# A decode kernel with two attention passes: K loads reordered behind the last fresh V, and the softmax bias from one row maximum

## The chip, the cores and the metric

The kernel runs on one core of a Trainium2 chip. The metric is device time in microseconds of one execution, as the median of the runs. A profile of one execution gives the trace that the numbers below come from. The engines are named as in the profile: PE (matrix multiply) with PEld (its weight loads), DVE (vector), ACT (scalar), POOL (GpSimd), and SP, whose queue issues the DMAs.

## What is computed

Four tokens (batch 4, one position each, width 448) go through attention over a cached window, then a gated feed-forward, and both once more with the same weights and the same cache:

```python
x = A_x
x = x + _A_ref(_layernorm(x, axis=-1), A_k_cache, A_v_cache, A_wq, A_wo)
x = x + _B_ref(_layernorm(x, axis=-1), B_w_gate, B_w_up, B_w_down)
x = x + _A_ref(_layernorm(x, axis=-1), A_k_cache, A_v_cache, A_wq, A_wo)
x = x + _B_ref(_layernorm(x, axis=-1), B_w_gate, B_w_up, B_w_down)
```

In the attention, 16 query heads of 256 share 8 KV heads, and the window is the last 2048 positions of the cache:

```python
scores = jnp.einsum("bhqd,bhkd->bhqk", q, k) * (Dh ** -0.5)
p = _softmax(scores, axis=-1)
o = jnp.einsum("bhqk,bhkd->bhqd", p, v)
```

So one KV head of one token is 1 MB of K and 1 MB of V, and there are 32 such heads, to be read for layer 0 and again for layer 1 (the second pass).

## The kernel before

**Pairs.** The unit of work is a "pair" (token `t`, layer, KV head): 64 in all, numbered by `pos`. `orders()` and `steps()` interleave the second pass of a token with the first pass of the next token. The end of the list is: 52 is (3, 0, 7), the last one of layer 0; 53 to 55 are (2, 1, 0), (2, 1, 1), (2, 1, 2); 56 to 60 are (3, 1, 3) to (3, 1, 7); 61 to 63 are (3, 1, 0), (3, 1, 1), (3, 1, 2).

**Cells.** K and V of a pair come in two halves of 512 KB, each in one of `NPOOL` = 27 cells `half`. The last five heads of each token in layer 0 keep their K and V in the cells for the second pass (`KEEP_K`, `KEEP_V`), so 20 cells are held while a token waits for its second pass, and its other three heads are loaded again.

**One pair** runs as follows. A K half lands (L722) and is transposed in place by DVE (L727). PE computes the scores into PSUM bank S (L748), 104 rows by 128. Each row holds one of two query heads by the parity of the row, and rows between the groups are empty. DVE takes each row's maximum (L759), PE spreads the 104 maxima over all rows by a matmul (L762: the maxima as weights, 32 columns of the identity as data), DVE takes the maximum over even and over odd columns, negated (L766, two values), and multiplies these with a parity mask and sums them into the bias of this row (L770, one instruction with an accumulator, which the profile shows as two). ACT takes the exponential with that bias (L773), PE turns the weights (L783), ACT copies them (L790), PE and DVE sum them (L793, L798), PE multiplies by V (L806, 16 matmuls, in two groups of 8 by V half, loaded by L735), POOL takes the reciprocal of the sum (L816), ACT and DVE join two parts (L818, L820), PE flips them (L826), DVE scales them (L831), and PE applies the output projection (L850 when a token is complete, else L858).

**Between the layers**, a complete token goes through `rows` (ACT L652, DVE L654, PE L662, DVE L666), `residual` (L670), `norm` (DVE L436 and L439, PE L442, DVE L446 to L455, POOL L459 to L463), the feed-forward (`ffn_row` from L558, or `ffn` with L612, L623 to L629 and L639), again `norm`, and `qproj`: L496 (two groups for each half of the result), ACT L502, PE L512 in two turns, DVE L519 (the copy qS), PE L527, DVE L532 (the query copy qc), then POOL builds the masked query of a pair (L752).

**Order.** Every operation is entered into a graph with an engine, a planned duration and a due time (`rank`), and `Graph.schedule` makes one fixed order for each engine. It always takes, of the operations ready by its own planned times, the one with the earliest due time. A DMA into a cell takes the cell that comes free first, and waits for the operation that frees it. Due times matter here in three places: a K half has `pos - KLEAD` (2.2), a V half `pos + VLAG` (1.3), and the work between the layers has `pos - CROSS` (20). On the chip each engine then runs its list in order, and waits on semaphores for what other engines produce.

The planner's own times only decide the order; they are not times of the chip.

Of the kernel before, what the change touches and what calls it, by code (L numbers as in the profile page):

```python
# [5 lines left out]
ACT = mybir.ActivationFunctionType  # L6
ALU = mybir.AluOpType
AX = mybir.AxisListType
# [5 lines left out]
B = 4  # L14
# [16 lines left out]

KLEAD = 2.2
VLAG = 1.3
SLEAD = 2.5
# [4 lines left out]
NS = 2  # L39
# [5 lines left out]
ROWF = (0, 1, 2)  # L45
MMV = 0.034
TAIL = {"pe": 0.2, "dve": 0.12, "act": 0.15, "pool": 0.1, "sp": 0.05}

# [231 lines left out]
def build(nc, A_x, A_k_cache, A_v_cache, A_wq, A_wo, B_x, B_w_gate, B_w_up, B_w_down, out):  # L280
# [3 lines left out]
    with ExitStack() as es:  # L284
        def sb(name, shape, dt):
            return es.enter_context(nc.sbuf_tensor(name, shape, dt))
# [9 lines left out]
        onesb, qmask, osel, rsel = tiny[:, 0:1], tiny[:, 2:6], tiny[:, 6:8], tiny[:, 8:12]  # L296
        pmax = [tiny[:, 12 + s:13 + s] for s in range(NS)]
        tsel = sb("tsel", [128, 4, B], BF16)
        selt = [sb(f"selt{h}", [128, 2, 4, 2, 2], BF16) for h in range(2)]
        small = sb("small", [128, 11 + 6 * NS + 4 * NY + B + 4], FP32)  # L300
        rmask = small[:, 11 + 6 * NS + 4 * NY:11 + 6 * NS + 4 * NY + B]
        rvec = small[:, 11 + 6 * NS + 4 * NY + B:11 + 6 * NS + 4 * NY + B + 4]
        nmask = small[:, 9 + 2 * NS + 4 * NY:11 + 2 * NS + 4 * NY]
        nbias = small[:, 11 + 2 * NS + 4 * NY:11 + 6 * NS + 4 * NY]
        onesf, wrow, lomask = small[:, 0:1], small[:, 1:5], small[:, 5:6]
# [71 lines left out]
        for h in range(2):  # L377
# [5 lines left out]
        g.op(DVE, 0.2, R0, lambda e: e.tensor_reduce(  # L383
            nmask[:, :], idq[:, :, 0:4, :].rearrange("p q a n -> p n q a"), AX.XY, ALU.add), r=("identb",), w=("nmask",))
        for s_ in range(NS):
            g.op(DVE, 0.2, R0, lambda e, s_=s_: e.memset(Sb[s_][:, :], 0.0), w=(f"s{s_}",), bank=(f"S{s_}",))
            g.op(DVE, 0.2, R0, lambda e, s_=s_: e.memset(praw[s_][:, :], 0.0), w=(f"praw{s_}",))
# [44 lines left out]
        def norm(t, rank, x):  # L432
# [24 lines left out]
            def gp(emit, r, w, dur=0.25):  # L457
                g.op(POOL, dur, rank, emit, r=r, w=w)
# [3 lines left out]
               (k + "m", k + "e", k + "w", k + "v"), (k + "h",))  # L462
            gp(lambda e: e.tensor_tensor(s[:, 8:9], s[:, 5:6], expo[:, 0:1], op=ALU.pow), (k + "h", "expo"), (k + "r2",))  # L463

# [243 lines left out]
        seq = [p for s in steps() for p in s]  # L708
        assert len(seq) == 2 * B * HKV and len(set(seq)) == len(seq)
        k_held, v_held = {}, {}  # L710
        done = {}
        pos = -1

        def pair(pos, si, side, nside, t, layer, kvh):
            p_, s_, q_ = pos % NY, pos % NS, pos % NQ
            if layer == 1 and (t, kvh) in k_held:
                kc, kk = k_held.pop((t, kvh))
            else:
                kc, kk = [[], []], [f"k{pos}_{hf}" for hf in range(2)]
                ksrc = A_k_cache[t, kvh, s0:s0 + WIN, :].rearrange("(p j) d -> p (j d)", p=128)  # L720
                for hf, cell in enumerate(kc):
                    g.dma(pos - KLEAD, 1 << 19, lambda e, cell=cell, hf=hf: e.dma_start(  # L722
                        half[cell[0]][:, :], ksrc[:, 2048 * hf:2048 * hf + 2048]), None, w=(kk[hf],), run=4096, cell=cell)

                    def tr(e, cell=cell):
                        a = half[cell[0]][:, :].bitcast(UINT32).rearrange("p (k s) -> p k s", k=32)
                        return e.transpose(a, a)  # L727
                    g.op(DVE, 1.18, pos, tr, w=(kk[hf],))
# [12 lines left out]
            def scores(e):  # L741
# [13 lines left out]
                r=(f"qc{t}_{kvh}",) + tuple(f"qmask{a}" for a in range(4)), w=(f"qe{q_}",))  # L755
            o = g.op(PE, 0.8, pos - SLEAD, scores, r=tuple(kk) + (f"qe{q_}",), w=(f"s{s_}",), bank=(f"S{s_}",))
            if not keep_k:
                o.rel = tuple(kc)
            g.op(DVE, 0.21, pos, lambda e: e.tensor_reduce(  # L759
                pmax[s_][0:104, :], Sb[s_][0:104, 0:128], AX.X, ALU.max),  # L760
                r=(f"s{s_}",), w=(f"pmax{s_}",), bank=(f"S{s_}",))
# [8 lines left out]
            g.op(DVE, 0.2, pos, lambda e: e.scalar_tensor_tensor(  # L770
                out=nb[0:104, 2:4], in0=negm[s_][0:104, :], scalar=1.0, in1=nmask[0:104, :], op0=ALU.mult, op1=ALU.mult,
                accum_out=nb[0:104, 0:1]), r=(f"negm{s_}", "nmask"), w=(f"nb{s_}",))
# [45 lines left out]
            g.op(SCA, 0.28, pos, lambda e: e.activation(oh[pos % 2][:, :], Yb[p_][:, 256:512], ACT.Copy), r=(f"y{p_}",),  # L818
                 w=(f"oh{pos % 2}",), bank=(f"Y{p_}",))
            g.op(DVE, 0.4, pos, lambda e: e.scalar_tensor_tensor(  # L820
                out=oh[pos % 2][:, :], in0=oh[pos % 2][:, :], scalar=lomask[:, 0:1], in1=Yb[p_][:, 256:512], op0=ALU.mult,
                op1=ALU.subtract), r=(f"y{p_}", f"oh{pos % 2}", "lomask"), w=(f"oh{pos % 2}",), bank=(f"Y{p_}",))

            def flip(e):
# [5 lines left out]
            o_ = oT[si % 2]  # L830
            g.op(DVE, 0.09, pos, lambda e: e.tensor_tensor(  # L831
                o_[:, :, :, t], Yb[p_][:, 0:4].rearrange("p (d n) -> p d n", n=2),
# [138 lines left out]
```

## Time and profile before

| what | us |
|---|---|
| median of 13 runs | 325.72 (322.11 to 328.94) |
| the profiled execution | 327.79 |
| its span, first to last instruction | 325.7 |
| busy: PE, PEld, DVE, ACT, POOL | 224.3, 136.0, 212.3, 74.9, 88.9 |
| moved by DMA | 105.16 MB, mean 323 GB/s |

The page shows the span in 40 slices of 8.14 us; a digit is the busy share in tenths, PEclk the clock that PE was granted, GB/s what the DMA engines moved:

```profile
PE   1746464556368757679779757785887688779775
DVE  7396645663255669877567769876778875845432
PEclk9999999999998787757675875576958755557655
GB/s 281 361 402 393 392 398 394 394 396 325 350 395 292 309 390 394 346 396 392 386 203 348 404 400 363 380 371 400 263 342 344 403 386 394 192 72 254 4 1 2
```

Transfers run near 390 GB/s for most of the span and drop at four places; the last five slices move next to nothing. PE runs at full clock at first and often at half of it later. The costliest groups (line, engine, operation, out and in, count, then busy us, mean ns of one, then the idle time before them and what ended it) begin with:

```profile
L727 DVE STREAM_TRANSPOSE half<-half 128x1024 uint32<-128x1024 uint32 x88 | 108.9, 1238 | 21.7 <-DMA half<-in_A_k_cache_dram 21.3
L806 PE MATMUL Y<-half,pT 128*4 128x256 bf16 x1024 | 62.1, 356 | 24.3 <-DMA half<-in_A_v_cache_dram 17.4
L748 PE MATMUL S<-half,qe 128*8 128x128 bf16 x2048 | 58.2, 278 | 6.3 <-DVE half L727 3.1
```

One transpose takes 1.24 us of DVE, which is long beside most other instructions there. The mean durations of PE overlap, as matmuls are pipelined.

### The profile page before, as it was taken

The page shows a single profiled execution, that of the slowest core. Times are in us where ns is not written, and L with a number is a line of the kernel's source. Part 1 is how long each engine was busy: PE and PEld are TensorE (multiplying, and loading weights), DVE is VectorE, ACT ScalarE, POOL GpSimd, SP SyncE. Part 2 cuts the span into 40 slices and gives each one's busy share as a digit, 9 for nine tenths or more (in the row PEclk, how much of TensorE's full clock was granted, in tenths as well). Part 3 has the DMA queues.
Part 4 walks back from the last instruction along what each step waited for, and adds up shares of the span by engine and source line. Part 5 has one row for each costly group of instructions (what it writes and reads, how often), then busy time and mean ns, then how long its engine had stood idle before and what let it go on. Part 6 is the DMA issues. An engine that isn't in the chain of part 4 may idle for free.

```text
span 325.7 us, 11153 instructions
## 1 busy us (share of the span) xinstructions
PE 224.3 (69%) x4776; PEld 136.0 (42%) x4776; DVE 212.3 (65%) x776; ACT 74.9 (23%) x222; POOL 88.9 (27%) x227
## 2 busy tenths in 40 slices
PE   1746464556368757679779757785887688779775
PEld 0334232223134435344346544443455446346444
DVE  7396645663255669877567769876778875845432
ACT  0122112111013223213232323131323322023210
POOL 1613211113010333223214323322243323225220
PEclk9999999999998787757675875576958755557655
DMA  7999999999997899999969999999799999526000
GB/s 281 361 402 393 392 398 394 394 396 325 350 395 292 309 390 394 346 396 392 386 203 348 404 400 363 380 371 400 263 342 344 403 386 394 192 72 254 4 1 2
DMA packets 42370, 105.16 MB, mean 323 GB/s; under 512 B 3145, under 2 KB 7249, under 8 KB 41937
## 3 DMA queue, kind: packets, MB, share of 16 engines
q1 hardware_dynamic: 42320, 104.45, 86.3%
q8 instruction: 37, 0.61, 0.7%
q14 instruction: 13, 0.10, 0.1%
HBM read 104.44 MB, written 0.00 MB: 321 GB/s over the span
## 4 chain that ended last, share of the span: by engine, by line
DMA 43%; PE 23%; SPq 16%; DVE 13%; issue 3%; ACT 1%; POOL 0%; DVEq 0%
DMA half<-in_A_k_cache_dram 23%; DMA half<-in_A_v_cache_dram 15%; DVE half L727 7%; PE Y L806 6%; SPq L735 6%; PE S L748 6%; SPq L722 6%; SPq L407 4%; DMA wg_sb<-in_B_w_gate_dram 4%; DVE oh L820 2%; PE Z L612 2%; PE A L858 2%; PE Z L558 1%; PE Z L496 1%; PE Y L826 1%
## 5 line engine op out<-in xcount | busy, mean ns | idle before, releaser
L727 DVE STREAM_TRANSPOSE half<-half 128x1024 uint32<-128x1024 uint32 x88 | 108.9, 1238 | 21.7 <-DMA half<-in_A_k_cache_dram 21.3
L806 PE MATMUL Y<-half,pT 128*4 128x256 bf16 x1024 | 62.1, 356 | 24.3 <-DMA half<-in_A_v_cache_dram 17.4
L816 POOL TENSOR_TENSOR small<-small 128x2 f32<-128x2 f32 x64 | 44.2, 695 | 80.5 <-DVE small L798 72.9
L748 PE MATMUL S<-half,qe 128*8 128x128 bf16 x2048 | 58.2, 278 | 6.3 <-DVE half L727 3.1
L748 PEld LDWEIGHTS S<-half,qe 128*8 128x8 bf16 x2048 | 44.7, 108 | 12.5 <-DVE half L727 4.4
L752 POOL TENSOR_TENSOR qe<-qc,tiny 128x64 bf16<-128x64 bf16 x64 | 18.6, 292 | 91.7 <-PE S L748 69.9
L818 ACT ACTIVATE oh<-Y 128x256 bf16<-128x256 f32 x64 | 24.5, 382 | 78.1 <-PE Y L806 77.9
L806 PEld LDWEIGHTS Y<-half,pT 128*4 128x4 bf16 x1024 | 21.7, 93 | 39.0 <-DMA half<-in_A_v_cache_dram 21.6
L773 ACT ACTIVATE praw<-S,small 104x128 bf16<-104x128 f32 x64 | 23.0, 366 | 63.5 <-DVE small L770 63.2
L820 DVE SCALAR_TENSOR_TENSOR oh<-oh,small,Y 128x256 bf16<-128x256 bf16 x64 | 30.0, 470 | 8.8 <-ACT oh L818 7.9
L759 DVE TENSOR_REDUCE tiny<-S 104x1 bf16<-104x128 f32 x64 | 18.4, 287 | 23.9 <-PE S L748 23.7
L826 PE MATMUL Y<-tiny,oh 128*128 128x2 bf16 x128 | 12.9, 172 | 18.9 <-DVE oh L820 17.9
L790 ACT ACTIVATE pT<-Y 128x64 bf16<-128x64 f32 x64 | 14.0, 222 | 40.2 <-PE Y L783 37.6
L858 PE MATMUL A<-wo_sb,oT 128*4 128x448 bf16 x140 | 17.2, 484 | 4.3 <-DVE oT L831 4.1
L826 PEld LDWEIGHTS Y<-tiny,oh 128*128 128x128 bf16 x128 | 8.3, 108 | 28.3 <-DVE oh L820 24.7
L783 PE MATMUL Y<-selt,praw 104*128 104x32 bf16 x256 | 17.3, 187 | 1.0 <-ACT praw L773 0.9
L793 PE MATMUL Y<-pT,tiny 128*128 128x32 bf16 x64 | 12.5, 197 | 7.9 <-ACT pT L790 7.8
L783 PEld LDWEIGHTS Y<-selt,praw 104*128 104x128 bf16 x256 | 11.8, 105 | 12.7 <-issue 9.4
L762 PE MATMUL S<-identb,tiny 104*104 104x32 bf16 x64 | 14.5, 241 | 2.9 <-DVE tiny L759 2.6
L766 DVE TENSOR_REDUCE small<-S 104x2 f32<-104x32 f32 x64 | 11.4, 183 | 6.5 <-PE S L762 6.3
L459 POOL TENSOR_SCALAR st<-st 128x1 f32<-128x1 f32 x16 | 4.2, 265 | 38.7 <-DVE st L448 38.7
L496 PE MATMUL Z<-wq_sb,xn 128*4 128x512 bf16 x120 | 13.9, 593 | 1.4 <-DVE st L448 1.4
(120 smaller groups left out, 243.0 us busy)
## 6 DMA issues: line engine op xcount, KB each, us to landing
half<-in_A_k_cache_dram SPq DMA_DIRECT2D x88, 512.0 KB, 7.7
half<-in_A_v_cache_dram SPq DMA_DIRECT2D x88, 512.0 KB, 7.6
wo_sb<-in_A_wo_dram SPq DMA_DIRECT2D x8, 448.0 KB, 12.7
wq_sb<-in_A_wq_dram SPq DMA_DIRECT2D x3, 1024.0 KB, 6.9
wd_sb<-in_B_w_down_dram SPq DMA_DIRECT2D x1, 1568.0 KB, 18.2
wg_sb<-in_B_w_gate_dram SPq DMA_DIRECT2D x1, 1344.0 KB, 15.1
wu_sb<-in_B_w_up_dram SPq DMA_DIRECT2D x1, 1344.0 KB, 15.4
wq_sb<-in_A_wq_dram SPq DMA_DIRECT2D x2, 256.0 KB, 9.9
```

Source lines behind the costliest of these rows:

```text
L722: g.dma(pos - KLEAD, 1 << 19, lambda e, cell=cell, hf=hf: e.dma_start(half[cell[0]][:, :], ksrc[:, 2048 * hf:2048 * hf + 2048]), None, w=( ...
L727: return e.transpose(a, a)
L735: g.dma(pos + VLAG, 1 << 19, lambda e, cell=cell, hv=hv: e.dma_start(half[cell[0]][:, :].rearrange("p (a g d) -> p a g d", a=2, g=4), vsrc ...
L748: last = e.matmul(Sb[s_][qd:qd + 8, 0:128], lhsT=qe[q_][:, ce, :, :].rearrange("p a n -> p (a n)"), rhs=kt[:, ce // 2, ce % 2, 2 * x:2 * x ...
L773: g.op(SCA, 0.38, pos, lambda e: e.activation(praw[s_][0:104, 2:258].rearrange("p (g r h l) -> p h g r l", g=2, h=2, l=2)[:, 0, :, :, :], ...
L783: last = e.matmul(Yb[p_][:, 64 + 32 * c:96 + 32 * c], lhsT=praw[s_][0:104, c0:c0 + 128], rhs=selt[h][0:104, :, :, :, :].rearrange("p x a y ...
L806: last = e.matmul(Yb[p_][32 * gg:32 * gg + 4, 256:512], lhsT=pT[p_][:, gg % 2, gg // 2, 2 * hv + a, :, :].rearrange("p y n -> p (y n)"), r ...
L816: g.op(POOL, 0.25, pos, lambda e: e.tensor_tensor(ri[p_][:, :], rs[p_][:, :], expo[:, 1:3], op=ALU.pow), r=(f"rs{p_}", "expo"), w=(f"ri{p_ ...
L818: g.op(SCA, 0.28, pos, lambda e: e.activation(oh[pos % 2][:, :], Yb[p_][:, 256:512], ACT.Copy), r=(f"y{p_}",), w=(f"oh{pos % 2}",), bank=( ...
L820: g.op(DVE, 0.4, pos, lambda e: e.scalar_tensor_tensor(out=oh[pos % 2][:, :], in0=oh[pos % 2][:, :], scalar=lomask[:, 0:1], in1=Yb[p_][:, ...
L826: last = e.matmul(Yb[p_][:, 2 * dh:2 * dh + 2], lhsT=oh[pos % 2][:, :].rearrange("p (m e) -> p e m", e=2)[:, dh, :], rhs=osel[:, :], start ...
L858: last = e.matmul(Ab[32 * k:32 * k + B, 0:D], lhsT=oT[si % 2][:, k % 2, k // 2, :], rhs=wo_sb[:, 4 * kvh + k, :], start=False, stop=False, ...
```

## The change

There are three parts.

1. **K of the tail.** For pairs after `LAST1` = 52, the last pair of layer 0, the due time of a K half is `pos + KTAIL` (0.4) instead of `pos - KLEAD`. Pairs 53, 54, 55, 61, 62 and 63 load K there, two halves each. The SP queue before has, from the V of pair 48 on, K52, K53, V50, K54, K55, V52, V53, V54, V55, K61, K62, K63, V61, V62, V63; the changed one has K52, V50, V52, K53, V53, K54, V54, K55, V55, K61, V61, K62, V62, K63, V63. Before that point the queue has the same order of transfers as before.
2. **The bias.** L766 now takes one maximum over all 32 columns of a row, and its negation is the bias. So that the columns of the other parity don't count, a matmul in front of L762 writes a mask into the same PSUM columns (identity as weights, `far` as data), and L762 adds to it: 0 where the column's parity is that of the row, -1e30 where not, +1e30 on empty rows. L770 and its buffer go. Three setup instructions on DVE build `far` from the parity mask `nmask`.
3. **Planned durations** of several operations, which change the order that the planner makes on all engines: scores 0.8 to 0.87, L759 0.21 to 0.23, L806 0.385 to 0.43 for each half, L816 0.25 to 0.69, the power in `norm` 0.25 to 0.58, L818 0.28 to 0.34, L820 0.4 to 0.43, L831 0.09 to 0.12.

```diff
+KTAIL = 0.4
+FAR = 1e30
...
+        far = sb("far", [128, 16, 2], BF16)
...
+        g.op(DVE, 0.1, R0, lambda e: e.tensor_reduce(negm[0][:, 0:1], nmask[:, :], AX.X, ALU.add), r=("nmask",), w=("negm0",))
+        g.op(DVE, 0.1, R0, lambda e: e.tensor_scalar(negm[0][:, 1:2], negm[0][:, 0:1], -2.0, 1.0, op0=ALU.mult, op1=ALU.add),
+             r=("negm0",), w=("negm0",))
+        g.op(DVE, 0.1, R0, lambda e: e.tensor_scalar(
+            far[:, :, :], nmask[:, :].unsqueeze(1).broadcast_to([128, 16, 2]), negm[0][:, 1:2], FAR, op0=ALU.add, op1=ALU.mult),
+            r=("nmask", "negm0"), w=("far",))
...
+        LAST1 = max(i for i, p in enumerate(seq) if p[1] == 0)
...
-                    g.dma(pos - KLEAD, 1 << 19, lambda e, cell=cell, hf=hf: e.dma_start(
+                    g.dma(pos - KLEAD if pos <= LAST1 else pos + KTAIL, 1 << 19, lambda e, cell=cell, hf=hf: e.dma_start(
...
-            o = g.op(PE, 0.8, pos - SLEAD, scores, r=tuple(kk) + (f"qe{q_}",), w=(f"s{s_}",), bank=(f"S{s_}",))
+            o = g.op(PE, 0.87, pos - SLEAD, scores, r=tuple(kk) + (f"qe{q_}",), w=(f"s{s_}",), bank=(f"S{s_}",))
...
-            g.op(PE, 0.1, pos, lambda e: e.matmul(
-                Sb[s_][0:104, 128:160].rearrange("p (q x) -> p q x", q=4), lhsT=pmax[s_][0:104, 0:1].broadcast_to([104, 104]),
-                rhs=identb[0:104, :].rearrange("p (q x) -> p q x", q=4)[:, :, 0:8], start=True, stop=True,
-                skip_group_check=True), r=(f"pmax{s_}", "identb"), w=(f"m{s_}",), bank=(f"S{s_}",))
-            g.op(DVE, 0.16, pos, lambda e: e.tensor_reduce(
-                negm[s_][0:104, :], Sb[s_][0:104, 128:160].rearrange("p (k n) -> p n k", n=2), AX.X, ALU.max, negate=True),
+            def spread(e):
+                e.matmul(Sb[s_][0:104, 128:160], lhsT=identb[0:104, 0:104],
+                         rhs=far[0:104, :, :].rearrange("p k n -> p (k n)"), start=True, stop=False, skip_group_check=True)
+                return e.matmul(
+                    Sb[s_][0:104, 128:160].rearrange("p (q x) -> p q x", q=4),
+                    lhsT=pmax[s_][0:104, 0:1].broadcast_to([104, 104]),
+                    rhs=identb[0:104, :].rearrange("p (q x) -> p q x", q=4)[:, :, 0:8], start=False, stop=True,
+                    skip_group_check=True)
+            g.op(PE, 0.12, pos, spread, r=(f"pmax{s_}", "identb", "far"), w=(f"m{s_}",), bank=(f"S{s_}",))
+            g.op(DVE, 0.13, pos, lambda e: e.tensor_reduce(
+                negm[s_][0:104, 0:1], Sb[s_][0:104, 128:160], AX.X, ALU.max, negate=True),
                 r=(f"m{s_}",), w=(f"negm{s_}",), bank=(f"S{s_}",))
-            nb = nbias[:, 4 * s_:4 * s_ + 4]
-            g.op(DVE, 0.2, pos, lambda e: e.scalar_tensor_tensor(
-                out=nb[0:104, 2:4], in0=negm[s_][0:104, :], scalar=1.0, in1=nmask[0:104, :], op0=ALU.mult, op1=ALU.mult,
-                accum_out=nb[0:104, 0:1]), r=(f"negm{s_}", "nmask"), w=(f"nb{s_}",))
...
-                Sb[s_][0:104, 0:128].rearrange("p (g l r) -> p g r l", g=2, l=2), ACT.Exp, bias=nb[0:104, 0:1]),
-                r=(f"s{s_}", f"nb{s_}"), w=(f"praw{s_}",), bank=(f"S{s_}",))
+                Sb[s_][0:104, 0:128].rearrange("p (g l r) -> p g r l", g=2, l=2), ACT.Exp, bias=negm[s_][0:104, 0:1]),
+                r=(f"s{s_}", f"negm{s_}"), w=(f"praw{s_}",), bank=(f"S{s_}",))
...
-                o = g.op(PE, 0.385, pos, lambda e, hv=hv: pv(e, hv), r=(f"pT{p_}", f"v{t}_{kvh}_{hv}"),
+                o = g.op(PE, 0.43, pos, lambda e, hv=hv: pv(e, hv), r=(f"pT{p_}", f"v{t}_{kvh}_{hv}"),
...
-            g.op(POOL, 0.25, pos, lambda e: e.tensor_tensor(
+            g.op(POOL, 0.69, pos, lambda e: e.tensor_tensor(
                 ri[p_][:, :], rs[p_][:, :], expo[:, 1:3], op=ALU.pow), r=(f"rs{p_}", "expo"), w=(f"ri{p_}",))
```

More of the change, by code (lines that the diff above doesn't have):

```diff
@@ L297, in build @@
         pmax = [tiny[:, 12 + s:13 + s] for s in range(NS)]
+        far = sb("far", [128, 16, 2], BF16)
         tsel = sb("tsel", [128, 4, B], BF16)
         selt = [sb(f"selt{h}", [128, 2, 4, 2, 2], BF16) for h in range(2)]
-        small = sb("small", [128, 11 + 6 * NS + 4 * NY + B + 4], FP32)
-        rmask = small[:, 11 + 6 * NS + 4 * NY:11 + 6 * NS + 4 * NY + B]
-        rvec = small[:, 11 + 6 * NS + 4 * NY + B:11 + 6 * NS + 4 * NY + B + 4]
+        small = sb("small", [128, 11 + 2 * NS + 4 * NY + B + 4], FP32)
+        rmask = small[:, 11 + 2 * NS + 4 * NY:11 + 2 * NS + 4 * NY + B]
+        rvec = small[:, 11 + 2 * NS + 4 * NY + B:11 + 2 * NS + 4 * NY + B + 4]
         nmask = small[:, 9 + 2 * NS + 4 * NY:11 + 2 * NS + 4 * NY]
-        nbias = small[:, 11 + 2 * NS + 4 * NY:11 + 6 * NS + 4 * NY]
         onesf, wrow, lomask = small[:, 0:1], small[:, 1:5], small[:, 5:6]
@@ L462, in norm @@
                (k + "m", k + "e", k + "w", k + "v"), (k + "h",))
[L463 removed]
+            gp(lambda e: e.tensor_tensor(s[:, 8:9], s[:, 5:6], expo[:, 0:1], op=ALU.pow), (k + "h", "expo"), (k + "r2",), 0.58)
         def rowvec(dst, key, ts, rank):
@@ L755, in pair @@
                 r=(f"qc{t}_{kvh}",) + tuple(f"qmask{a}" for a in range(4)), w=(f"qe{q_}",))
-            o = g.op(PE, 0.8, pos - SLEAD, scores, r=tuple(kk) + (f"qe{q_}",), w=(f"s{s_}",), bank=(f"S{s_}",))
+            o = g.op(PE, 0.87, pos - SLEAD, scores, r=tuple(kk) + (f"qe{q_}",), w=(f"s{s_}",), bank=(f"S{s_}",))
             if not keep_k:
                 o.rel = tuple(kc)
-            g.op(DVE, 0.21, pos, lambda e: e.tensor_reduce(
+            g.op(DVE, 0.23, pos, lambda e: e.tensor_reduce(
@@ L815, in pair @@
                     o.rel = (vs[hv],)
-            g.op(POOL, 0.25, pos, lambda e: e.tensor_tensor(
+            g.op(POOL, 0.69, pos, lambda e: e.tensor_tensor(
                 ri[p_][:, :], rs[p_][:, :], expo[:, 1:3], op=ALU.pow), r=(f"rs{p_}", "expo"), w=(f"ri{p_}",))
-            g.op(SCA, 0.28, pos, lambda e: e.activation(oh[pos % 2][:, :], Yb[p_][:, 256:512], ACT.Copy), r=(f"y{p_}",),
+            g.op(SCA, 0.34, pos, lambda e: e.activation(oh[pos % 2][:, :], Yb[p_][:, 256:512], ACT.Copy), r=(f"y{p_}",),
                  w=(f"oh{pos % 2}",), bank=(f"Y{p_}",))
-            g.op(DVE, 0.4, pos, lambda e: e.scalar_tensor_tensor(
+            g.op(DVE, 0.43, pos, lambda e: e.scalar_tensor_tensor(
                 out=oh[pos % 2][:, :], in0=oh[pos % 2][:, :], scalar=lomask[:, 0:1], in1=Yb[p_][:, 256:512], op0=ALU.mult,
@@ L830, in pair @@
             o_ = oT[si % 2]
-            g.op(DVE, 0.09, pos, lambda e: e.tensor_tensor(
+            g.op(DVE, 0.12, pos, lambda e: e.tensor_tensor(
                 o_[:, :, :, t], Yb[p_][:, 0:4].rearrange("p (d n) -> p d n", n=2),
```

## The prediction

> **What bounds the kernel now.** I read the span by stages first, because whole-span shares (PE 69%, DVE 65%) mix stages. Stretches of the trace, cut where the transfers stop and resume (columns: stretch, its length, busy time and instructions of PE, PEld, DVE, ACT, POOL, clock, DMA share, GB/s):
>
> ```profile
> 163.00:175.00 12.00, 9.76 (x254) 6.78 (x250) 8.07 (x37) 3.33 (x9) 3.52 (x11) 0.64 0.73 263
> 175.00:228.00 53.00, 39.02 (x871) 24.23 (x863) 41.52 (x140) 14.62 (x45) 16.68 (x39) 0.66 1.01 380
> 228.00:244.00 16.00, 13.17 (x326) 8.53 (x322) 11.72 (x45) 5.22 (x14) 5.57 (x16) 0.71 0.84 299
> 244.00:278.00 34.00, 27.41 (x686) 18.61 (x679) 25.67 (x93) 9.81 (x32) 11.04 (x24) 0.65 1.01 381
> 278.00:290.00 12.00, 8.56 (x152) 4.33 (x152) 7.43 (x27) 2.19 (x4) 2.10 (x8) 0.50 0.27 100
> 299.00:325.70 26.70, 18.92 (x439) 12.28 (x427) 10.25 (x55) 5.22 (x18) 6.09 (x12) 0.60 0.02 5
> ```
>
> At 380 GB/s the kernel is bound by its transfers. Three holes break that: at 163 to 175 (3.16 MB that need 8.3 us at 380 GB/s take 12, so 3.7 us lost), at 228 to 244 (4.78 MB, 3.4 us lost) and at 278 to 290. After 299 there is nothing left to load. The holes are where a token passes from layer 0 to its second pass: its feed-forward and query projection must end before the K halves it holds can be scored and their cells freed. In the last hole the sync queue shows it (L735's six last V halves are issued over 14.81 us):
>
> ```profile
> 249.48 4.74 SPq L722 DMA_DIRECT2D half<-in_A_k_cache_dram  x4
> 254.57 12.74 SPq L735 DMA_DIRECT2D half<-in_A_v_cache_dram  x8
> 267.35 12.09 SPq L722 DMA_DIRECT2D half<-in_A_k_cache_dram  x6
> 279.54 14.81 SPq L735 DMA_DIRECT2D half<-in_A_v_cache_dram  x6
> ```
>
> Then the chain that ended last, from the landing of the last layer-0 V (token 3, head 7) on:
>
> ```profile
> 254.57 9.26 DMA half<-in_A_v_cache_dram
> ...
> 267.77 0.52 PE A L850 x16
> ...
> 282.23 1.44 PE Z L496 x12
> ...
> 289.05 1.81 PE S L748 x48
> ```
>
> So V lands at 263.83, its second half's product runs at 265.20 to 265.79, token 3's last output projection at 267.77, its query projection at 282.23, and the first score of its second pass at 288.98 (in the PE timeline). From there to the output's DMA at 324.05 are 35.1 us of work that PE fills to about 85%. What the change can win in the tail is what it takes from 263.8 to 289. There DVE runs six K transposes of pairs 61 to 63 in front of chain steps:
>
> ```profile
> 276.46 1.24 DVE L727 STREAM_TRANSPOSE half<-half 128x1024 uint32<-128x1024 uint32 x1
> 277.67 1.22 DVE L727 STREAM_TRANSPOSE half<-half 128x1024 uint32<-128x1024 uint32 x1
> 279.20 1.24 DVE L727 STREAM_TRANSPOSE half<-half 128x1024 uint32<-128x1024 uint32 x1
> 280.80 1.24 DVE L727 STREAM_TRANSPOSE half<-half 128x1024 uint32<-128x1024 uint32 x1
> ```
>
> The down projection ended at 278.1, its residual came at 278.82; the two norm steps around 279.2 are split by the next transpose (1.15 us), and the norm's matmul, over at 281.1, is read only at 281.96 (0.85). That is 2.7 us of chain.
>
> **What the Trainium skill says.** "PSUM — Partial Sum Buffer", Engine vs sequencer instructions: Vector queues are strict FIFO and matmuls start and complete in program order. The trace agrees: DVE sat 4.32 us before a transpose at 164.57, while the query copy L519, ready since about 165.15, went after it at 165.74. "TensorE: Matmul & The Clock Gate", LDWEIGHTS and Back-to-back issue gap, prices the added matmul: 104 columns / 1.2 is an estimate of 87 ns for the weights and 32 / 1.2 of 27 ns for the product at the slow clock. The trace has 0.09 to 0.10 us for the twin L762 where it follows other work, so it agrees; I use that.
>
> **Part 1, the bias.** Per pair it removes L770, two DVE instructions:
>
> ```profile
> L770 DVE SCALAR_TENSOR_TENSOR small<-small 104x2 f32<-104x2 f32 x64 | 9.4, 152 | 0.4
> L770 DVE DVE_READ_ACCUMULATOR small<-small 104x1 f32 x64 | 5.2, 82 | 0.0
> ```
>
> By start-to-start times they take about 0.15 us of DVE, so 64 x 0.15 = 10 us of 212; in the latency of one pair 0.24 us. The reduce L766 (183 ns) keeps its place and reads all 32 columns into one value; 0 to -0.03 each. Added is one matmul of 104x104 by 104x32, in front of L762 and behind the same wait, so no new wait: 0.03 (weights hidden) to 0.11 us each; I take 0.05 in a filled PE, 0.1 in the latency. Net latency per pair -0.15. In the body DVE is the busiest beside the transfers but these cover it: I count nothing for the 10 us. PE pays: about 14 pairs lie in the two catch-up stretches, 14 x 0.05 = +0.7; the tail's eight pairs, 8 x 0.05 to 0.1 = +0.4 to 0.8, against some 0.3 won before the first exponential. Tail: +0.3. Three setup instructions on DVE lie in the first 10 us, under the first loads.
>
> **Part 2, the planner's costs** (scores 0.87, POOL power 0.69, and so on) cost nothing themselves but move instructions. The built program's order shows where. For token 1, query projection now stands ahead of the product that waits for V (PE idle 1.01 before 159.32) and its xn step ahead of the transpose at 157.34 (1.24), and the copy L519 no longer stands behind the transpose of 164.57. Projection 158.3 instead of 159.99, query written 164.9 instead of 166.73 to 166.93: -1.8 us, of which the hole's 3.7 us can give back most; I take -1.2 (bounds 0 and -1.8). For token 2 the row turn L662 comes ahead of the product that waited 1.41 us at 224.49; projection at about 224.6 instead of 228.21. But on DVE the transpose that landed at 229.70 now stands between L519 and the query copy L532: 229.7 + 0.55 (L654) + 0.40 (L820) + 1.25 puts it at 232.2 instead of 233.30. -1.0 (bounds +0.5 and -1.4). For token 0 one transpose moves ahead of the query copy and scores 14 and 11 swap; both end near 105.7 as before: 0.
>
> **Part 3, the K halves.** Twelve 512 KB halves (pairs 53, 54, 55, 61, 62, 63) move behind the last fresh V on the SP queue and now alternate with the V of the same pair; twelve transposes on DVE and six score groups on PE move with them. POOL's queue is not passed. Landing times: transfer 167 of that queue (counted from 0 over all of them; K52's first half) landed at 249.64, transfer 177 (V52's first half) at 263.83, so 1.42 us each; to the eighth after it (274.54) 1.34. V52, the last fresh V, becomes 171 and 172: 255.3 and 256.7, 8.5 us earlier. The chain does not follow that far, since K53, K54, K55 now land within it. Step by step, by the built order:
> K53's first half lands at 258.2 and is transposed ahead of the row step L654; the turn and pair 52's V product come at 260.5 to 261.6 (before, to 265.79). K53's scores stand ahead of the flip L826: second half 259.6, transposed to 261.9, scored to 262.9; the column projection runs at 263.4 (before 267.77): -4.3. K54 lands at 263.8 and 265.1; its transposes split residual and norm, and its scores stand ahead of the norm's matmul: 267.7 (before 268.97): -1.3. The feed-forward runs unbroken from 269.5 to 273.1. K55's scores stand before the down projection; its second half is issued only when pair 54 is scored (267.7) and lands at about 271.5 (3.3 us is the least time to landing in the trace, I take 3.8), transposed to 273.3: down at 274.4 (before 276.51): -2.1. Behind it DVE has one transpose instead of four: norm matmul 277.4 (before 280.55): -3.1. The projection starts at 278.7; its edge rows wait for K61's second half (issued at 274.4, landed 278.1, transposed 279.5) and run at 280.5 (before 284.05). Pair 55's V products and two DVE steps (0.95) precede the query copy: first score at 286.2 instead of 288.98, -2.8. The seven unheld cells (27 less the 20 that hold five K and five V) are full by then in both orders, and five halves remain in both: they took 290 to 299 and were needed from 303.7 on, so the later K63 is covered by 5 us or more; without cover, a late K63 would cost its excess one for one.
>
> **Sum.** -2.8 + 0.3 (tail) - 1.2 - 1.0 + 0.7 = -4.0 us. The profiled execution took 327.79 with a span of 325.7, so its span would be 321.7. The median of the runs, 325.72, is 2.07 below that execution; the same difference from it gives **321.7 us**, its own range 319 to 324.
>
> **The rivals.**
> *A, slower: the chain now waits for transfers.* Two loops are new between 265 and 280: K55 issued after score 54, K61 after score 55, each with in-order DVE and PE queued behind: down projection, norm, projection. I gave each 3.7 to 3.8 us to landing; the median in the trace is 7.6. Each us more is paid twice: from 5.7 us on the gain is gone; at 6.8 us it is +2.1, 327.8. For it: the spread of landings. Against it: while the queue waits for cells, few transfers are in flight.
> *B, no change.* The first-pass orders win nothing, as the transfers hide them, and each loop takes 1 us more: -2.5 + 2.0 = -0.5 plus 0.7, some 325.9 us.
> *C, larger gain.* The two body holes close by half and more (3.5 instead of 2.2 us) and the lighter DVE shortens the norm chains: 318.5.
> That the change does not do what it says is ruled out for the SP queue, whose built order has the V first.
>
> **How the numbers follow.** About 0.5% (1.6 us) is what a measurement can tell from no change. Forecast 0.57, A 0.18, B 0.14, C 0.11. Faster is forecast and C, 0.68; same 0.14; slower 0.18. Range 317.5 to 327: it takes in C, B and A's near half.
>
> **What would show it.** Right: product L806 of pair 52 done near 261.6, first score of pair 56 near 286 less what the body won; the holes near 165 and 230 shorter by about 1 us; L770 gone; the stretch from that first score to the output still about 35 us. Wrong: DVE or PE waiting more than 2 us for K between that product and the projection, or later holes as wide as before.

## The result

| | before | changed |
|---|---|---|
| median of the runs, us | 325.71 (48 runs, 321.55 to 329.18) | 321.32 (11 runs, 316.98 to 322.77) |
| ratio, 95% interval | | 0.986 (0.982 to 0.990) |
| the profiled execution, its span | 327.79, 325.7 | 318.71, 316.6 |

The change takes 4.4 us off the median; the forecast was 4.0, to 321.7. Executions of one kernel differ by 2% and more: the ratio and its interval compare only those within 1.5% of the fastest of their kernel, the medians are over all, so the two can differ.

The two profiled executions differ by 9.1 us, which is twice the gain. The one of before shown above lies 2.1 us above the median of its runs. A second trace of before (321.98 us, span 319.9), which lies 3.7 us below it, is therefore compared with the changed kernel below.

### The profile page after: what moved, and what is told of

Read it like the earlier page. It is cut to its first block, busy times and chain, and to the rows that moved or that the text cites. A ratio compares the mean times of both kernels' runs of the same rounds, so it can differ in the third digit from the quotient of the medians.

```text
span 316.6 us, 11163 instructions
## 1 busy us (share of the span) xinstructions
PE 224.0 (71%) x4840; PEld 137.9 (44%) x4840; DVE 207.0 (65%) x651; ACT 76.5 (24%) x222; POOL 89.0 (28%) x227
## 4 chain that ended last, share of the span: by engine, by line
DMA 45%; PE 23%; SPq 17%; DVE 11%; issue 3%; ACT 1%
DMA half<-in_A_k_cache_dram 21%; DMA half<-in_A_v_cache_dram 19%; SPq L744 7%; DVE half L736 6%; SPq L731 6%; PE Y L816 6%; PE S L757 6%; SPq L415 4%; DMA wg_sb<-in_B_w_gate_dram 4%; PE Z L504 2%; PE Z L566 2%; DVE oh L830 1%; PE A L868 1%; PE Z L620 1%; PE Y L793 1%
## 5 line engine op out<-in xcount | busy, mean ns | idle before, releaser
L816 PE MATMUL Y<-half,pT 128*4 128x256 bf16 x1024 | 60.0, 352 | 16.2 <-DMA half<-in_A_v_cache_dram 13.4
L757 PE MATMUL S<-half,qe 128*8 128x128 bf16 x2048 | 56.7, 272 | 13.2 <-DVE half L736 9.2
L757 PEld LDWEIGHTS S<-half,qe 128*8 128x8 bf16 x2048 | 42.7, 105 | 19.3 <-DVE half L736 11.5
L768 DVE TENSOR_REDUCE tiny<-S 104x1 bf16<-104x128 f32 x64 | 18.4, 287 | 26.0 <-PE S L757 25.6
L816 PEld LDWEIGHTS Y<-half,pT 128*4 128x4 bf16 x1024 | 21.7, 93 | 29.0 <-DMA half<-in_A_v_cache_dram 17.9
L836 PE MATMUL Y<-tiny,oh 128*128 128x2 bf16 x128 | 13.0, 172 | 12.4 <-DVE oh L830 11.8
L868 PE MATMUL A<-wo_sb,oT 128*4 128x448 bf16 x140 | 16.5, 460 | 4.5 <-DVE oT L841 3.9
L793 PEld LDWEIGHTS Y<-selt,praw 104*128 104x128 bf16 x256 | 11.3, 103 | 13.9 <-issue 8.9
L772 PE MATMUL S<-far,identb 104*104 104x32 bf16 x64 | 14.9, 238 | 3.3 <-DVE tiny L768 2.1
L780 DVE TENSOR_REDUCE small<-S 104x1 f32<-104x32 f32 x64 | 11.5, 183 | 7.5 <-PE S L774 5.1
L467 POOL TENSOR_SCALAR st<-st 128x1 f32<-128x1 f32 x16 | 4.2, 264 | 36.6 <-DVE st L456 36.5
```

The source lines that it names most:

```text
L757: last = e.matmul(Sb[s_][qd:qd + 8, 0:128], lhsT=qe[q_][:, ce, :, :].rearrange("p a n -> p (a n)"), rhs=kt[:, ce // 2, ce % 2, 2 * x:2 * x ...
L793: last = e.matmul(Yb[p_][:, 64 + 32 * c:96 + 32 * c], lhsT=praw[s_][0:104, c0:c0 + 128], rhs=selt[h][0:104, :, :, :, :].rearrange("p x a y ...
L816: last = e.matmul(Yb[p_][32 * gg:32 * gg + 4, 256:512], lhsT=pT[p_][:, gg % 2, gg // 2, 2 * hv + a, :, :].rearrange("p y n -> p (y n)"), r ...
L836: last = e.matmul(Yb[p_][:, 2 * dh:2 * dh + 2], lhsT=oh[pos % 2][:, :].rearrange("p (m e) -> p e m", e=2)[:, dh, :], rhs=osel[:, :], start ...
L868: last = e.matmul(Ab[32 * k:32 * k + B, 0:D], lhsT=oT[si % 2][:, k % 2, k // 2, :], rhs=wo_sb[:, 4 * kvh + k, :], start=False, stop=False, ...
```

## The profile after

The 40 slices of the changed kernel, clock and transfers:

```profile
PEclk9999999999999657959585967585955955576995
GB/s 279 357 405 393 393 395 396 395 393 329 314 396 317 321 399 399 389 397 370 396 355 369 372 408 397 383 328 391 341 296 337 396 383 293 239 221 321 16 3 3
```

The deepest holes of the first trace of before are filled: its 21st slice had 203 GB/s, here 355, and its 192, 72 and 254 near the end are now 239, 221 and 321. (Of the last five slices of before only three move next to nothing.) The loads of the tail are spread instead of stopped. The same three stretches as in the prediction, first from the second trace of before, then from the changed kernel (stretch, length, busy time and instructions of PE, PEld, DVE, ACT, POOL, clock, DMA share, GB/s):

```profile
163.00:175.00 12.00, 9.89 (x246) 7.27 (x246) 9.25 (x45) 3.11 (x10) 4.84 (x13) 0.60 0.87 295
228.00:244.00 16.00, 13.42 (x322) 9.60 (x318) 11.50 (x50) 4.58 (x15) 6.15 (x16) 0.57 0.87 311
278.00:290.00 12.00, 8.52 (x154) 4.79 (x153) 6.19 (x29) 2.19 (x5) 3.47 (x12) 0.50 0.32 113
```

```profile
163.00:175.00 12.00, 8.78 (x246) 6.78 (x246) 8.99 (x29) 3.18 (x10) 4.01 (x12) 0.72 0.98 358
228.00:244.00 16.00, 14.17 (x318) 9.50 (x319) 11.31 (x38) 4.37 (x14) 6.87 (x17) 0.53 0.90 320
278.00:290.00 12.00, 10.57 (x251) 7.22 (x247) 6.91 (x27) 3.79 (x10) 4.71 (x16) 0.64 0.70 245
```

At 380 GB/s, the first hole won 12 x (358 - 295) / 380 = 2.0 us, the second 16 x (320 - 311) / 380 = 0.4 us. So in these two executions the body gained more at token 1 and less at token 2 than forecast.

The tail is read from the chain that ended last (start, length, what):

```profile
261.57 1.04 PE S L757 x18
262.63 0.34 SPq L731
...
264.83 7.29 DMA half<-in_A_k_cache_dram
272.14 1.25 DVE half L736
273.43 0.07 DVE xs L655
...
283.98 0.38 SPq L744
284.40 5.70 DMA half<-in_A_k_cache_dram
290.12 1.25 DVE half L736
```

The 7.29 us are the first half of K61, from issue to landing, the 5.70 us that of K63. In the first trace of before, the last load on the chain was a V of layer 0. In its second trace one K follows that V, and it is K61's first half as well:

```profile
264.23 7.43 DMA half<-in_A_k_cache_dram
```

The DVE timeline of the changed kernel shows what stood behind K (start, length, operation; in brackets the idle time before it and what ended it):

```profile
272.14 1.25 DVE L736 STREAM_TRANSPOSE half<-half 128x1024 uint32<-128x1024 uint32 x1 [2.34 <-DMA half<-in_A_k_cache_dram]
273.31 0.12 DVE L655 TENSOR_TENSOR xr<-xr,Z 128x4 f32<-128x4 f32 x1
...
279.76 1.25 DVE L736 STREAM_TRANSPOSE half<-half 128x1024 uint32<-128x1024 uint32 x1 [1.99 <-DMA half<-in_A_k_cache_dram]
281.03 0.19 DVE L527 CAST qS<-Z 128x32 bf16<-128x32 f32 x1
```

The down projection (L647) ran from 269.38 to 271.0, but its residual L655 came only at 273.31: it stood behind the transpose of K61, for which DVE waited 2.34 us. This is the strict FIFO of the Vector queue that the Trainium skill names ("PSUM — Partial Sum Buffer", Engine vs sequencer instructions). The 1.99 us before K62 cost little, as qS's input ended at about 281.0.

Before, DVE also waited for K61, but for less long, and then had the four transposes that the prediction shows between the down projection and the end of the norm. In the first trace of before:

```profile
274.56 1.25 DVE L727 STREAM_TRANSPOSE half<-half 128x1024 uint32<-128x1024 uint32 x1 [0.89 <-DMA half<-in_A_k_cache_dram]
```

That load had been issued at 267.35, so it took 7.2 us there.

## The experiments

A stage table carries most of them. Its marks are starts in the timelines: the query copy of token 2 (L540 in the changed kernel), the column projection of pair 52 (L860), the query copy of token 3, the output's DMA. Each row is one execution, us from mark to mark. The number in brackets is the part of its stage from the down projection of token 3 (L647) on.

| kernel | execution | to query of token 2 | to projection of 52 | to query of token 3 | to output |
|---|---|---|---|---|---|
| before | 327.79 | 233.3 | 34.4 | 20.4 (11.6) | 35.9 |
| before, second trace | 321.98 | 229.5 | 35.1 | 20.6 (11.6) | 33.0 |
| bias alone | 324.88 | 231.6 | 35.7 | 20.2 (11.6) | 33.7 |
| order alone | 322.87 | 227.1 | 38.7 | 20.0 (11.3) | 33.3 |
| order and bias | 320.83 | 226.7 | 36.6 | 20.6 (11.7) | 33.2 |
| K move alone | 327.47 | 235.2 | 31.7 | 23.5 (13.5) | 33.5 |
| changed | 318.71 | 226.6 | 32.4 | 23.1 (12.7) | 32.9 |
| changed, again | 319.41 | 227.1 | 33.1 | 22.0 (12.2) | 33.6 |
| old bias, new order | 323.01 | 228.1 | 32.8 | 23.3 (12.4) | 35.1 |
| mask ahead | 322.92 | 229.6 | 33.2 | 23.5 (13.5) | 33.1 |
| mask twice | 322.52 | 226.5 | 34.3 | 23.1 (13.2) | 34.8 |
| K behind the chain | 321.11 | 227.9 | 32.5 | 21.3 (11.6) | 35.9 |
| K behind the chain, 2 | 318.92 | 226.6 | 33.0 | 20.7 (10.8) | 34.9 |
| K behind the chain, 3 | 321.10 | 226.6 | 33.7 | 22.0 (10.4) | 35.0 |

**The K move alone.** Only the due time of the K halves is changed in the kernel before:

```diff
-                    g.dma(pos - KLEAD, 1 << 19, ...
+                    g.dma(pos - KLEAD if pos <= LAST1 else pos + KTAIL, 1 << 19, ...
```

> The kernel before with the due time of the tail's K halves alone changed (order before pair 52 as before, bias as before). My theory (three parts of about equal weight): the tail's chain gives 2.8 us, no bias term and no body term, so ratio 0.9915 (322.9 against 325.7). Rival 'the K move is the whole gain': ratio 0.985 to 0.987, 4.2 to 4.9 us. Rival 'the tail only waits elsewhere': within 0.4% of before, with DVE waiting 2 us for K61 and K62 in front of chain steps.

Measured: 0.9968 (0.9938 to 0.9998), medians 324.12 and 324.45. By the ratio that is 1.0 us (0.1 to 2.0), by the medians 0.3; the forecast of 2.8 lies outside either way. The third rival, that the tail only waits elsewhere, is the one that fits. DVE in its timeline:

```profile
280.13 1.25 DVE L729 STREAM_TRANSPOSE half<-half 128x1024 uint32<-128x1024 uint32 x1 [2.74 <-DMA half<-in_A_k_cache_dram]
281.30 0.12 DVE L648 TENSOR_TENSOR xr<-xr,Z 128x4 f32<-128x4 f32 x1
...
288.13 1.25 DVE L729 STREAM_TRANSPOSE half<-half 128x1024 uint32<-128x1024 uint32 x1 [2.38 <-DMA half<-in_A_k_cache_dram]
289.40 0.19 DVE L520 CAST qS<-Z 128x32 bf16<-128x32 f32 x1
```

The same two waits, on the old order and with the old bias: they belong to the K move. In the stage table the six kernels with the move and no other order of transposes (K move alone to mask twice) reach the projection of 52 early, 31.7 to 34.3 us against 34.4 to 38.7, and give 1.4 to 3.5 us back on the way to the query (22.0 to 23.5 against 20.0 to 20.6). From the down projection on they take 12.2 to 13.5 us, the kernels without the move 11.3 to 11.7.

**The bias alone**, in the order of before. L770 stays in the plan as an entry that emits nothing:

```diff
+            g.op(DVE, 0.2, pos, None, r=(f"negm{s_}", "nmask"), w=(f"nb{s_}",))
...
+        for o in self.ops:
+            for d in [d for d in o.deps if d.emit is None]:
+                o.deps.pop(d)
...
```

> The kernel before with the new bias alone; L770 stays in the plan as a ghost, so that the order of all other instructions is that of before (but for a few in the first four pairs). My theory, as predicted: nothing from DVE, +0.7 us in the catch-up stretches and +0.3 in the tail for the matmul: ratio 1.003 (1.000 to 1.004). Rival 'the 0.15 us per pair taken off DVE closes the holes between tokens': 2 to 3 us faster, ratio 0.990 to 0.994.

Measured: 1.0071 (1.0030 to 1.0112), medians 326.46 and 324.45: slower by 2.3 us. The rival, that the lighter DVE closes the holes, falls. The size is more than the 1.0 us of the prediction. In this execution the loss stands ahead of the query of token 2 (231.6 against 229.5 us).

**The order alone.** The changed kernel's durations, the order that they and the new bias's durations give, with the old bias instructions in it:

```diff
+            g.second[o] = lambda e: e.scalar_tensor_tensor(
+                out=nb[0:104, 2:4], in0=negm[s_][0:104, :], scalar=1.0, in1=nmask[0:104, :], ...
...
+            order[e] = [y for o in order[e] for y in ((o, behind[o]) if o in behind else (o,))]
```

> The order of instructions that the new planned durations give (those of the bias among them), with the old bias instructions in it (L770 directly behind its reduce) and the old due times of K. My theory: token 1's and token 2's query projections come earlier, -1.2 and -1.0, so 2.2 us faster, ratio 0.993 (0.990 to 1.000). Rival 'the order wins nothing since transfers hide it': ratio 1.000 within 0.3%. If the order closes the holes nearly whole: 4 us, ratio 0.988.

Measured: 0.9931 (0.9903 to 0.9960), medians 322.59 and 324.45: 2.2 us, as forecast. Its first two stretches:

```profile
163.00:175.00 12.00, 7.49 (x184) 5.54 (x172) 9.12 (x35) 2.53 (x8) 3.63 (x11) 0.65 0.94 332
228.00:244.00 16.00, 12.57 (x296) 8.44 (x284) 10.59 (x46) 4.14 (x13) 5.39 (x15) 0.50 0.71 249
```

Token 1's query copy starts at 161.6 there instead of 164.4, and the first hole is partly closed, 332 GB/s against 295. But the second is wider, 249 against 311, and the projection of 52 comes at 265.8, later than the 264.6 of the second trace of before. So the runs show the 2.2 us, and the trace shows the earlier queries; how these reach the output, this execution does not show.

**Order and bias**, that is, the changed kernel without the K move (`pos - KLEAD` for all).

> The changed kernel with the old due time of the tail's K halves, so parts 2 and 3 of the change without part 1 of it. My theory: -2.2 + 1.0 = 1.2 us faster than before, ratio 0.996, with the first score of pair 56 about 35 us ahead of the output as before. Rival 'the body is the whole gain': ratio 0.986 to 0.988, the same as the whole change. Rival 'K is the whole gain': ratio 1.000 or above.

Measured: ratio 0.9977 (0.9947 to 1.0006), but medians of 322.25 and 324.45, equal to the order alone within 0.4 us. The two readings differ by 1.5 us, so the ratio decides little. The 22 runs of each have means of 322.22 us (this) and 322.25 us (order alone), so on the new order no cost of the bias can be told. Its trace has the first score 21.5 us behind the projection, and 32.4 us ahead of the output. This is also the fitting control for the K move on the new order: from the query of token 2 to that of token 3 it takes 57.2 us, the changed kernel 55.5 and 55.1.

**The changed kernel again**, measured beside the next three kernels:

> The changed kernel itself, for its ratio in the same job as the next three: 0.986 (0.982 to 0.990) as first measured. If the parts simply added, the runs of the parts would give 0.9977 x 0.9968 = 0.9945; a ratio of 0.986 again means that the K move is worth about 1.2% on the new order and 0.3% on the old one.

Measured: 0.989 (0.983 to 0.995), medians 320.95 and 324.00. The product of the three parts alone is 0.9968 x 1.0071 x 0.9931 = 0.997. The whole is better by 2.6 us (from 0.989) or 3.6 us (from 0.986): the parts, each alone on the old kernel, don't add. Each factor has an interval of 0.3 to 0.4% to either side, so the first of the two differences lies at the edge of what can be told, the second beyond it.

**The old bias in the new order**: the changed kernel with L770 back, directly behind its reduce, and without the mask matmul.

> The changed kernel with the old bias (L770 back, no mask matmul), in the changed kernel's own order of instructions, L770 directly behind its reduce. My theory after the first four runs (the bias costs time on PE, 64 x 0.083 us, of which about half shows): 1 to 2 us faster than the changed kernel, ratio to before 0.980 to 0.983. Rival 'the bias shortens the tail's pairs': 0.5 to 1 us slower than the changed kernel, 0.988 to 0.990.

Measured: 0.9889 (0.9856 to 0.9921), medians 322.86 and 324.00; against 0.989 of the changed kernel beside it, so no difference can be told by the ratio. The first expectation missed. The ratio lies where the rival put it, but the rival took the changed kernel at 0.986. The medians differ by 1.9 us (322.86 and 320.95, the latter of six runs between 319.2 and 327.1), so a small saving by the new bias is not excluded.

**The mask matmul ahead of the scores**, in front of their wait for K:

```diff
+            g.ahead[o] = lambda e: e.matmul(
+                Sb[s_][0:104, 128:160], lhsT=identb[0:104, 0:104],
+                rhs=far[0:104, :, :].rearrange("p k n -> p (k n)"), start=True, stop=False, skip_group_check=True)
```

The same matmul goes out of `spread`.

> The changed kernel in its own order, but the mask matmul stands in front of the scores of its pair, before their wait for K, instead of behind the row maximum. The same PE work, 0.08 us less between row maximum and exponential. If the bias's cost is that latency: ratio 0.981 to 0.983, and as fast as the old bias. If it is PE's time as such: the same as the changed kernel within 0.3%. If PE's idle time before K covers it: between the two.

Measured: 0.9823 (0.9754 to 0.9892), but medians of 322.84 and 324.00 over six runs between 317.6 and 325.4; the ratio rests on two of them. Inconclusive.

**The mask matmul twice**, the changed kernel otherwise:

> The changed kernel, its own order, with the mask matmul issued twice (the same result), so 64 x 0.08 = 5.2 us more of PE, on no other engine anything. It separates the bias's two halves. 'PE's added time is what the bias costs, as it seemed on the old order (+2 us)': about 2 us slower than the changed kernel, ratio to before 0.993 to 0.996. 'On the new order PE has slack for it': within 0.3% of the changed kernel, 0.985 to 0.990; then nothing of the change's gain or loss is due to that matmul.

Measured: 0.9876 (0.9809 to 0.9942), medians 322.01 and 325.43. Its groups (busy us, mean ns of one):

```profile
L772 PE MATMUL S<-far,identb 104*104 104x32 bf16 x64 | 15.5, 242 | 2.1 <-DVE tiny L768 2.0
L774 PE MATMUL S<-far,identb 104*104 104x32 bf16 x64 | 14.9, 233 | 0.0
```

64 more matmuls change nothing that these runs can tell (the interval is as wide as 4 us); the ratio lies in the second range and outside the first, into which its interval reaches. The mean of 240 ns is the length of a pipelined one; from start to start the changed kernel's L772 and its successor are 0.08 us apart. With the old bias in the new order, which won nothing by the ratio, this speaks for slack on PE in the new order; it does not prove it. Why the bias costs 2 us on the old order stays open. That its order was planned for another bias is one thought, and was not tried.

**K behind the chain.** In the changed kernel the transposes of K61 are ordered behind the second norm of token 3, those of K62 behind the copy qS ("xe3" is the last piece of that norm's result):

```diff
+DEFER = {(61, 0): ("xe3",), (61, 1): ("xe3",), (62, 0): ("qS",), (62, 1): ("qS",)}
...
-                    g.op(DVE, 1.18, pos, tr, w=(kk[hf],))
+                    g.op(DVE, 1.18, pos, tr, r=DEFER.get((pos, hf), ()), w=(kk[hf],))
```

> The changed kernel with the transposes of pair 61 ordered behind the second norm of token 3 and those of pair 62 behind the copy qS, so that the DVE waits of 2.34 and 1.99 us stand no longer in front of chain steps. If those waits ate the tail's gain (my theory): the residual of the down projection comes 1.2 us behind that product instead of 2.3, the first score of pair 56 some 1.8 us earlier, ratio 0.979 to 0.982. Rival 'the next K is what the chain needs anyway': pairs 61 to 63 come late by as much, ratio 0.986 within 0.3%.

Measured: 0.9856 (0.9809 to 0.9902), medians 320.02 and 324.00. Projection to first score fell to 22.0 us. But in this order the first score stands ahead of the last projection of token 2, so about 1 us of PE work passes to the other side of that mark; the query of token 3 is the fairer one, 21.3 us against 22.0 and 23.1. The ratio missed the expectation and lies in the rival's range. The last stage rose to 35.9. Two gaps stand in its PE timeline, in the middle of groups:

```profile
275.11 0.59 PE L817 MATMUL Y<-half,pT 128*4 128x256 bf16 x7 [1.42 <-issue]
288.84 0.39 PE L758 MATMUL S<-half,qe 128*8 128x128 bf16 x8 [2.48 <-issue]
```

"issue" is time in which PE waited for nothing that the profile shows. The first lies in the stage that became shorter. The second is the larger part of the 2.3 to 3.0 us by which the last stage is longer than in the changed kernel, whose own two traces have gaps of 0.36 and 1.12 us in that stage.

**The same, a step further**: K61's first half behind the norm, its second half behind qS, K62 behind the query copy ("qc3_0"):

```diff
-DEFER = {(61, 0): ("xe3",), (61, 1): ("xe3",), (62, 0): ("qS",), (62, 1): ("qS",)}
+DEFER = {(61, 0): ("xe3",), (61, 1): ("qS",), (62, 0): ("qc3_0",), (62, 1): ("qc3_0",)}
```

> The first K half of pair 61 transposed behind the second norm of token 3, its second half behind the copy qS, both of pair 62 behind the query copy. In the earlier run with this idea the second half of K61 (1.23 us) stood in front of the scaling of pair 54's output, and the second query turn waited 0.79 us behind it. My theory (K transposes in front of chain steps are what the tail loses): column projection to first score 20 to 21.5 us, where the changed kernel took 24.1 and 23.1; ratio 0.977 to 0.983. Rival 'later K costs it back': first score to output grows from 32 to 34 us or more with DVE or PE waiting for K61 to K63, ratio 0.986 to 0.990.

Measured: 0.9833 (0.9779 to 0.9886), medians 318.95 and 325.43: the lowest median of all. DVE in its timeline:

```profile
271.20 0.16 DVE L656 TENSOR_TENSOR xr<-xr,Z 128x4 f32<-128x4 f32 x1 [1.27 <-PE Z L648]
...
275.21 1.25 DVE L737 STREAM_TRANSPOSE half<-half 128x1024 uint32<-128x1024 uint32 x1
...
278.89 0.19 DVE L528 CAST qS<-Z 128x32 bf16<-128x32 f32 x1 [0.78 <-PE Y L804]
```

The residual now follows its product at once (in the changed kernel it came 2.1 us later, from a projection of 52 that was 0.6 us earlier), and no wait for K stands before qS. Projection to query is 20.7 us, as without the K move; to the first score 21.4. From the down projection to the query it takes 10.8 us instead of 12.7 and 12.2. So the loss in front of the query is what the waits for K cost there: shown by taking them away. The last stage is 34.9 us, 1.3 to 2.0 above the changed kernel's, and the first score stands 34.2 us ahead of the output, which is the size that the rival named, though with gaps put down to issue (1.48 and 0.83) and not with waits for K. So this one execution is no faster in sum. That the kernel beats the one before is shown. That it beats the changed one is not: it was not measured beside it, its median is 2.0 to 2.4 us lower where before took 325.43, and the intervals of the ratios overlap.

**And further still**, both halves of K61 behind qS:

> As the kernel before it, but both K halves of pair 61 are transposed behind the copy qS, so that pair 61 is scored behind pair 60 and the cells that it frees come later. If the K in front of the chain is still the loss: column projection to first score 20.5 to 21.4 us, ratio 0.977 to 0.983. Rival 'the cover of the late K is used up': first score to output 34 us or more, with waits for K63 in it, ratio 0.985 to 0.990.

Measured: 0.9853 (0.9794 to 0.9912), medians 320.74 and 325.32. More delay brings nothing more, and the ratio missed the expectation and lies in the rival's range. Projection to first score is 22.7, but that is not K61's doing: DVE waited ahead of the down projection, for the second half of K55.

```profile
269.65 1.25 DVE L737 STREAM_TRANSPOSE half<-half 128x1024 uint32<-128x1024 uint32 x1 [1.60 <-DMA half<-in_A_k_cache_dram]
```

From the down projection on it has the shortest way to the query of all, 10.4 us. From the first score to the output it takes 34.3 us, but PE's timeline has no wait for a K of pairs 61 to 63 in it, and only one gap, of 0.30. Two things differ in the last stage of all three kernels of this kind. One or two of the deferred transposes, 1.25 us each, now stand in it. And PE was granted a clock of 0.71 to 0.74 there, against 0.78 in both traces of the changed kernel: it was busy for 26.4 to 27.5 us with nearly the same matmuls, against 25.6 and 25.7. In the third kernel that is most or all of the 1.4 to 2.1 us. Whether the deferred transposes bring the longer stage with them, so that the time is only moved, was not tried.

**The kernel before, once more:**

> The kernel before once more, for stage lengths out of a second trace: second query copy (token 2) to the column projection of pair 52 34.4 us, from there to the first score of pair 56 21.3, from there to the output 32 to 35, as in the first trace. If the new waits are what lengthens the middle stage, it is 21 to 22 here and 23 to 25 in every kernel with the K move.

Measured: one run, 321.98 us. The middle stage is 21.5, as expected if the K move lengthens it, and 23.1 to 24.7 in the six kernels with the move and no deferred transposes; the last stage is 32.1, not 35.1.

## Why the prediction was right, and where it was not

The forecast of -4.0 us met -4.4. Of its terms the order held; the K halves fell short, and the bias did not cost what was forecast. These two made up for each other, so that the sum came so close is in part luck. One of the forecast's own signs of being wrong came true as well: DVE waited more than 2 us for K between the product of pair 52 and the projection (2.34 us; 1.50 in the changed kernel's other trace).

- **Order, -2.2: right.** Alone it gives 2.2 us. The query of token 1 was forecast 1.8 us earlier with 1.2 counted; in the changed kernel's two traces it is 2.1 and 1.3 (162.3 and 163.1, from 164.4). Token 2 was forecast to add 1.0; it adds 0.8 and 1.1. The sum behind that 1.0 was off: 229.7 + 0.55 + 0.40 + 1.25 is 231.9, not 232.2, which would have made it 1.4. The way from the queries to the output was argued and is not shown.
- **K halves, -2.8: the direction right, the size not.** By the runs the move alone is worth 0.3 to 1.0 us; on the new order it is more, 1.7 to 2.0 us between the two queries by the traces. The step that failed is "Behind it DVE has one transpose instead of four". That transpose is K61's first half. The forecast gave its second half 3.7 us to land and took the first as landed. It was issued at 264.83, right behind three other halves (262.63 to 264.3), took 7.29 us, and held the residual. So from the down projection to the second norm's matmul it was 5.1 us (269.38 to 274.46) instead of 3.0; the steps around it were near the forecast (projection to down projection 10.4 for 11.0, norm to query projection 1.3 for 1.3, from there to the first score 7.4 for 7.5). The first trace of before had the warning: the same half took 7.2 us there, and DVE waited 0.89 us for it.
- **Also in that term:** the projection of 52 was to come 4.3 us earlier. With the move alone the stage before it is 2.7 us shorter than in the first trace of before (31.7 from 34.4), on the new order 3.4 to 4.2 (33.1 and 32.4 from 36.6).
- **Why the loss is K's:** ordering the transposes behind the chain makes the way from the down projection to the query 10.4 to 11.6 us, from 12.2 to 13.5. That makes the cause shown there, not argued. It is not shown that the whole kernel gets faster by it.
- **Bias, +1.0: wrong on either order.** Alone on the old order it costs 2.3 (1.0 to 3.6); on the new order nothing that can be told. The price of the mask was 0.08 us each instead of 0.05. The reduce stayed at 183 ns, as taken. DVE's busy sum fell from 214.8 to 206.3 between order alone and order and bias, near the 10 us of the estimate, and no run shows a gain from it, as forecast.
- **Cover of the late K63, "5 us or more": wrong, and it cost nothing visible.** K63's first half landed at 290.1 and stands on the chain, since its transpose stands in DVE's order ahead of other steps; first score to output is 31.8 and 32.5, against 32.1.
- **"Still about 35 us" from first score to output: wrong**, but not by the change: the 35.1 belonged to the first trace of before; its second has 32.1. In the first, PE's granted clock from the query of token 3 to the output was 0.59, in the second 0.71.
- **The rivals.** A ends on the wrong side. Of its two loops the first is real: K55's second half, issued at 262.63, came for 267.12 and cost DVE 0.51 us of waiting (1.60 in one other kernel). The second, K61's second half behind score 55, shows no wait; the first half does. B (no change) falls with the result, and C's lighter DVE with the bias alone. The parts alone sum to some 3 us less than the whole; about the size of what the bias costs on the old order and not on the new one. The cause of that cost is open.

## What to carry to other kernels

A load moved behind more urgent ones arrives in time only if its own time to landing is counted as the trace has it at that place (7.2 us here), not near the least one in the trace (3.3 us). On an engine that runs its list in order, as DVE did here, the step that needs the late data must then also move behind the steps that don't: look for each transpose or copy in front of the chain and ask what it waits for. Where several parts are changed at once, try each alone and in the final order: the bias cost 2 us in one order here, and nothing that could be told in the other.

## What the runs showed of the hardware that was not expected

On the changed kernel's chain three 512 KB halves took 8.84, 7.29 and 5.70 us from issue to landing, the last while the stretch from 278 to 290 us moved only 245 GB/s. In some executions PE paused 1.0 to 2.5 us ahead of or within a group of matmuls without a wait that the profile shows (1.42 and 2.48 in one trace, 1.04 and 1.84 near 252 us in the two of the changed kernel, none above 0.5 in the second trace of before). The granted clock of one stage differs between executions of one kernel (0.59 and 0.71 in the last stage of before). So single traces of one kernel can differ by 3 us in a stage (35.9 and 33.0 there).
